# Rounding copies of the spatial weights on ScalarE instead of VectorE, in a fused recurrence and gated-MLP kernel

## The chip, the cores and the metric

The kernel runs on one core of a Trainium2 chip. The metric is the device time of one execution in microseconds (us). The engines of a core have a queue each and work through it in order: TensorE multiplies matrices (in the rows of the profile PE, its weight loads PEld), VectorE is DVE, ScalarE is ACT, GpSimd is POOL, and SyncE (SP) issues the transfers. An instruction that waits holds up everything behind it in the queue of its engine.

## The reference, cut to what matters

A recurrence over 768 tokens for 4 batches and 8 heads, each with a 40 by 40 state, is followed by a gated MLP whose gate mixes tokens with a 768 by 768 matrix, `w_spatial`.

```python
for t in range(S):                                   # S = 768
    y[:, :, t] = np.einsum('bhd,bhde->bhe', rt, state)
    Sa = np.einsum('bhde,bhe->bhd', state, at)
    state = state * wt[:, :, None, :] - np.einsum('bhd,bhe->bhde', Sa, bt) \
            + np.einsum('bhd,bhe->bhde', vt, kt)
x = y.transpose(0, 2, 1, 3).reshape(B, S, H * D)
h = np.maximum(x @ w_in, 0.0)
u, v = h[..., :512], h[..., 512:]
v_n = (v - mu) / np.sqrt(var + 1e-06)
v_s = np.einsum('ts,bsd->btd', w_spatial, v_n) + b_spatial[None, :, None]
return (u * v_s) @ w_out
```

## The kernel before

**First phase.** The recurrence is cut into blocks of 64 tokens. 24 blocks (12 for each of two pairs of batches) go one after the other. Within a block the chain is: product with the state (`c_bp`, matmuls L908) and its copy out of PSUM on ScalarE (`c_bp_out`, L917), a product with the block's triangular matrix (`c_ff`, L925) and its copy (`c_ff_out`, L933), a product with the inverted block matrix (`c_xx`, L946) and its copy (`c_xx_out`, L957), a triangular mask by GpSimd (`strict`, L762), and the new state (`c_mp`, L976, finished on VectorE in L993 and L994) and the output (`c_y`, L1002, L1015). For the block after, ScalarE copies in between what is prepared: `b_lka_out` (`At`, L772), `b_tok_out` (L813), `b_l21_out` (L833), `b_zt_out` (`zt`, L853), `b_xcopy` (L1145). The input layer of the MLP is woven in, 12 units of 128 tokens and two batches: matmuls `m_u` (L1122) and `m_v` (L1076) into the PSUM tiles `pv` and, in the last units, `itmp`; ScalarE's Relu copies `m_u_out` (`ur`, L1128) and `m_v_out` (`vr`, L1082); statistics on VectorE (L1088 to L1106); the normalizing step on ScalarE (`m_n3`, L1111) and the store of `vr` to `vns`. `vr` has two buffers. The order of all of it is written out by hand in a table of numbers, one for each step.

**Second phase.** The spatial product is done with 2 by 2 quadrants in 7 products instead of 8. The weights are needed as 7 quadrants or combinations of quadrants, each split into a rounded part `wsh` and a remainder `wsl`, in fp32r, which TensorE takes. `wprep(i)` makes them for one of three slices of 128 source tokens: a load of `raw` (L311), four differences into `tt` on VectorE (L315), and then four times a rounding copy into `wsh` (L320) and the remainder `wsl` (L321), over 1, 2, 2 and 2 tiles of 384. The three calls are held behind marks in the first phase (places 20.03, 20.51 and 21.68 in units of blocks); from there, and for all that comes after the hand-written part, a scheduler of the framework places each instruction. `raw` has two buffers, which go on to the four chunks of `w_out` (`decode64`, L215 to L255: it makes fp32r pairs `woh` and `wol`) and then to the normalized activations (`vload`, L355, from `vns`). `product` (L402) then does the spatial matmuls, `gate` (L408, L206, L210) the gating and its split, and `proj` (L447, L448) the output layer.

`split_hi` (L206) is the helper that the other splits of the kernel use already; its rows all have line L206.

Of the kernel before, what the change touches and what calls it, by code (L numbers as in the profile page):

```python
# [204 lines left out]
def split_hi(eng, hi, x):  # L205
    eng.activation(hi, x, AF.Copy)  # L206
# [76 lines left out]
def phase2(ctx, tc, vns, uts, wspT, bsp, wout, out, anchors):  # L283
    nc = tc.nc
# [24 lines left out]
    def wprep(i):  # L309
        raw = wstg.tile([P, 2, S], F32, name="raw", bufs=2)  # L310
        nc.sync.dma_start(out=raw, in_=wspT.rearrange("(a k p) t -> k p a t", a=2, p=P)[i])  # L311
        r11, r12, r21, r22 = (raw[:, a, h * TH:(h + 1) * TH] for a in range(2) for h in range(2))
        tt = wstg.tile([P, 4, TH], F32, name="tt")
        for o, x, y in ((0, r12, r11), (1, r22, tt[:, 0]), (2, r22, r12), (3, r21, tt[:, 1])):
            nc.vector.tensor_tensor(out=tt[:, o], in0=x, in1=y, op=ALU.subtract)  # L315
        wh = wsp[2 * i].tile([P, 7, TH], F32R, name=f"wsh{i}")
        wl = wsp[2 * i + 1].tile([P, 7, TH], F32R, name=f"wsl{i}")
        for o, x in ((slice(0, 1), raw[:, 0:1, 0:TH]), (slice(1, 3), raw[:, 1].rearrange("p (h t) -> p h t", h=2)),
                     (slice(3, 5), tt[:, 0:2]), (slice(5, 7), tt[:, 2:4])):
            nc.vector.tensor_copy(out=wh[:, o], in_=x)  # L320
            nc.vector.tensor_tensor(out=wl[:, o], in0=x, in1=wh[:, o].bitcast(F32), op=ALU.subtract)  # L321
        wsh.append(wh)
        wsl.append(wl)

    for i in range(KT):
        sp = mybir.EngineType.SP
        with behind(tc, {**anchors[W_AT[i]], sp: anchors[W_AT[i] - W_LOAD][sp]}):
            wprep(i)
# [1055 lines left out]
```

## Time and profile before

| | us |
|---|---|
| median of 3 runs | 675.8 |
| lowest and highest run | 674.05, 679.77 |
| the profiled execution | 679.68 |
| its span, from the first instruction to the last | 678.0 |
| busy in it: TensorE, VectorE, ScalarE, GpSimd | 581.3, 518.0, 420.3, 208.0 |

How to read it: the profiled execution is one of those that scatter around the median. All times inside it are counted from the start of its span. A row of the timeline gives start, duration (of the whole stretch where several instructions are merged), engine, line, operation, output and input tiles with partitions and elements, the count, and in square brackets the idle time of the engine ahead of it with what ended it. Instructions overlap by their pipelines: the distance between two starts is shorter than the first one's duration. TensorE's granted clock was 1.00 of its full 2.4 GHz in every stretch from 440 us on that is looked at below but the last, with 0.99.

### The profile page before, as it was taken

The page shows a single profiled execution, that of the slowest core. Times are in us where ns is not written, and L with a number is a line of the kernel's source. Part 1 is how long each engine was busy: PE and PEld are TensorE (multiplying, and loading weights), DVE is VectorE, ACT ScalarE, POOL GpSimd, SP SyncE. Part 2 cuts the span into 40 slices and gives each one's busy share as a digit, 9 for nine tenths or more (in the row PEclk, how much of TensorE's full clock was granted, in tenths as well). Part 3 has the DMA queues.
Part 4 walks back from the last instruction along what each step waited for, and adds up shares of the span by engine and source line. Part 5 has one row for each costly group of instructions (what it writes and reads, how often), then busy time and mean ns, then how long its engine had stood idle before and what let it go on. Part 6 is the DMA issues. An engine that isn't in the chain of part 4 may idle for free. (4 is left out here: it accounts for less than half of the span.)

```text
span 678.0 us, 27119 instructions
## 1 busy us (share of the span) xinstructions
PE 581.3 (86%) x11504; PEld 512.6 (76%) x11504; DVE 518.0 (76%) x1110; ACT 420.3 (62%) x934; POOL 208.0 (31%) x286
## 2 busy tenths in 40 slices
PE   1736978878787887997999999989997989999996
PEld 1625866667676676886888888878876989999996
DVE  7871268779988999786899896793498779887842
ACT  3345454538485787786688889888864544443322
POOL 3201030133253445332135342434351113322221
PEclk9976597669796999999899999999999999999999
DMA  8383247276547464474754453655247744544201
GB/s 190 52 155 51 55 95 146 57 125 142 125 92 167 75 147 100 102 160 116 135 132 105 122 145 91 194 143 167 81 123 224 227 160 130 157 133 136 77 30 58
DMA packets 115496, 83.42 MB, mean 123 GB/s; under 512 B 44656, under 2 KB 107376, under 8 KB 113456
## 3 DMA queue, kind: packets, MB, share of 16 engines
q1 hardware_dynamic: 114832, 79.98, 48.4%
q10 hardware_dynamic: 544, 1.72, 1.2%
q8 instruction: 90, 1.47, 1.0%
q14 instruction: 30, 0.25, 0.2%
HBM read 61.16 MB, written 20.50 MB: 120 GB/s over the span
## 5 line engine op out<-in xcount | busy, mean ns | idle before, releaser
L762 POOL TENSOR_SCALAR_AFFINE_SELECT Rt<-Rt 64x256 f32<-64x256 f32 (+1 forms) x144 | 88.4, 615 | 175.9 <-ACT Rt L957 120.7
L762 POOL TENSOR_SCALAR_AFFINE_SELECT At<-At 64x512 f32<-64x512 f32 x48 | 36.1, 752 | 142.8 <-ACT At L772 138.8
L210 POOL TENSOR_TENSOR gl<-g,gh 128x384 fp32r<-128x384 f32 x32 | 34.9, 1091 | 104.2 <-ACT gh L206 104.2
L917 ACT ACTIVATE Rt<-bp 64x416 f32<-64x416 f32 x96 | 49.0, 511 | 23.6 <-PE bp L908 21.6
L957 ACT ACTIVATE Rt<-ch 64x416 f32<-64x416 f32 x96 | 49.1, 511 | 15.0 <-PE ch L946 13.1
L619 DVE TENSOR_TENSOR itmp<-A 128x84 f32<-128x84 f32 (+12 forms) x130 | 53.0, 408 | 2.5
L925 PE MATMUL ch<-Rt,At 128*64 128x104 f32 x768 | 47.3, 264 | 4.1 <-ACT Rt L917 1.8
L623 DVE TENSOR_TENSOR A<-A,itmp 128x84 f32<-128x84 f32 (+12 forms) x130 | 45.0, 346 | 4.5
L925 PEld LDWEIGHTS ch<-Rt,At 128*64 128x64 f32 x768 | 38.3, 141 | 11.1 <-ACT Rt L917 4.5
L946 PE MATMUL ch<-ffs,xf 64*64 64x104 f32 x768 | 39.8, 264 | 5.3 <-ACT ffs L933 4.8
L1015 DVE TENSOR_TENSOR y<-bp,Et 104x256 f32<-104x256 f32 x48 | 19.7, 418 | 32.1 <-ACT zt L853 18.0
L538 DVE TENSOR_TENSOR_SCAN S<-ein,ends 128x528 f32<-128x528 f32 x24 | 30.0, 1250 | 12.9 <-DMA ein<-in_early 9.6
L807 PE MATMUL bk<-ident,sl 128*128 128x128 f32 x192 | 34.6, 311 | 5.9 <-DVE Lc L595 2.4
L946 PEld LDWEIGHTS ch<-ffs,xf 64*64 64x64 f32 x768 | 31.4, 138 | 9.4 <-ACT ffs L933 6.0
L584 PE MATMUL bk<-at,sl 64*32 64x32 f32 x1536 | 21.8, 212 | 17.1 <-DVE sl L571 15.1
L206 ACT ACTIVATE gh<-g 128x384 fp32r<-128x384 f32 x32 | 16.7, 522 | 29.8 <-DVE g L408 29.8
L755 PE MATMUL bk<-at,sl 64*64 64x64 f32 x768 | 33.2, 248 | 1.1 <-issue 1.0
L584 PEld LDWEIGHTS bk<-at,sl 64*32 64x32 f32 x1536 | 18.8, 124 | 20.0 <-DVE sl L571 15.0
L402 PE MATMUL pg<-wsh,hs 128*128 128x384 f32 x96 | 32.3, 337 | 1.3 <-DVE g L408 1.3
L1002 PE MATMUL bp<-Rt,tk 128*40 128x64 f32 x768 | 32.6, 234 | 0.3 <-POOL Rt L762 0.2
L571 DVE TENSOR_TENSOR sl<-ein,S 128x1024 f32<-128x1024 f32 x24 | 30.1, 1255 | 3.6 <-PE bk L807 3.6
L772 ACT ACTIVATE At<-bk 64x512 f32<-64x512 f32 x48 | 28.2, 587 | 6.9 <-PE bk L755 6.2
(186 smaller groups left out, 1743.9 us busy)
## 6 DMA issues: line engine op xcount, KB each, us to landing
ein<-in_early SPq DMA_DIRECT2D x40, 387.0 KB
lin<-in_late SPq DMA_DIRECT2D x48, 160.0 KB
uts<-ur SPq DMA_DIRECT2D x48, 128.0 KB
vns<-vr SPq DMA_DIRECT2D x24, 256.0 KB
ut<-uts SPq DMA_DIRECT2D x48, 128.0 KB
raw<-vns SPq DMA_DIRECT2D x48, 128.0 KB
Rt<-in_vtok SPq DMA_DIRECT2D x48, 80.0 KB
xs<-y SPq DMA_DIRECT2D x48, 80.0 KB
```

Of the source, the lines that this page charges most:

```text
L210: eng.tensor_tensor(out=lo, in0=x, in1=hi.bitcast(F32), op=ALU.subtract)
L584: nc.tensor.matmul(pl[o:o + HB, n, :], lhsT=sl[PR[par], n, par, cs], rhs=at[PR[par], n, cs], start=True, stop=True,)
L619: nc.vector.tensor_tensor(out=tp, in0=A[:, k + 1:, k:k + 1].broadcast_to([P, m, k]), in1=A[:, k:k + 1, 0:k].broadcast_to([P, m, k]), op=AL ...
L623: nc.vector.tensor_tensor(out=A[:, k + 1:, 0:k], in0=A[:, k + 1:, 0:k], in1=tp, op=ALU.add)
L755: nc.tensor.matmul(pk[PR[1 - par], n, :], lhsT=sl[PR[par], n, 1 - par, :], rhs=at[PR[par], n, :], start=True, stop=True,)
L762: nc.gpsimd.affine_select(out=t, in_=t, pattern=[[0, k], [1, C]], base=0, channel_multiplier=-1, compare_op=ALU.is_gt, fill=0.0,)
L807: nc.tensor.transpose(pt[:, n, :], sl[:, h * NP + n].rearrange("p q c -> p (q c)"), ident)
L917: nc.scalar.activation(Rt[par][PR[par], gp, :], st["bp", g][PR[par]], AF.Copy)
L925: nc.tensor.matmul(ff[PR[1 - par], q, :], lhsT=At[par][:, n, :], rhs=Rt[par][:, n, :], start=True, stop=True,)
L946: nc.tensor.matmul(st["xx", g][PR[h ^ flip(s, g)], q, :], lhsT=xf[PR[h], g * NP + q, :], rhs=st["ffs", g][PR[h], q, :], start=True, stop=True,
L957: nc.scalar.activation(Rt[par][PR[par], gp], xx[PR[1 - par ^ flip(s, g)]], AF.Copy, scale=-1.0)
L1002: nc.tensor.matmul(bp[RR[par], q, 0:C], lhsT=tk[:, n, par, :], rhs=Rt[par][:, n, 0:C], start=False, stop=True, skip_group_check=True,)
```

## The change

One call in `wprep` is exchanged. The 12 rounding copies (4 in each of 3 calls) are issued on ScalarE as an activation with the copy function, and the subtraction that gives the remainder stays on VectorE.

```diff
         for o, x in ((slice(0, 1), raw[:, 0:1, 0:TH]), (slice(1, 3), raw[:, 1].rearrange("p (h t) -> p h t", h=2)),
                      (slice(3, 5), tt[:, 0:2]), (slice(5, 7), tt[:, 2:4])):
-            nc.vector.tensor_copy(out=wh[:, o], in_=x)
+            split_hi(nc.scalar, wh[:, o], x)
             nc.vector.tensor_tensor(out=wl[:, o], in0=x, in1=wh[:, o].bitcast(F32), op=ALU.subtract)
```

The scheduler places the new instructions. On GpSimd the order is the same as before. On TensorE and SyncE it is the same up to the last unit of the MLP's input layer, and in the part after it some pieces change places.

ScalarE, at the first call (`wsh_9573` is its output, `bp_7996` and `bp_7997` are the two PSUM tiles of `c_bp`); a piece of the difference:

```order
 L917 ACTIVATE Rt_132<-bp_7996 64x416
 L917 ACTIVATE Rt_133<-bp_7996 64x416
+L206 ACTIVATE wsh_9573<-raw 128x384
+L206 ACTIVATE wsh_9573<-raw 128x768
 L917 ACTIVATE Rt_132<-bp_7997 64x416
 L917 ACTIVATE Rt_133<-bp_7997 64x416
 L1145 ACTIVATE xf_130<-XT_7887 128x8x32
 L1145 ACTIVATE xf_130<-XT_7887 32x8x32 x2
+L206 ACTIVATE wsh_9573<-tt 128x768 x2
 L772 ACTIVATE At_8051<-bk 64x512
 L1097 ACTIVATE q<-q 128x1
```

Two copies now stand between the two pairs of L917, and two more ahead of the copy of `At`. The four copies of the second call stand in the same way between L1111 and L833 a little further on.

ScalarE, at the third call (`wsh_9607`), in the last block of the recurrence; before, and then now:

```order
L933 ACTIVATE ffs<-ch 128x416 x2
L1128 ACTIVATE ur<-pv 128x256
L1111 ACTIVATE vr<-vr,q 128x512
L957 ACTIVATE Rt_134<-ch 64x416
L957 ACTIVATE Rt_135<-ch 64x416
```

```order
L933 ACTIVATE ffs<-ch 128x416 x2
L206 ACTIVATE wsh_9607<-raw 128x384
L206 ACTIVATE wsh_9607<-raw 128x768
L206 ACTIVATE wsh_9607<-tt 128x768 x2
L1128 ACTIVATE ur<-pv 128x256
L1111 ACTIVATE vr<-vr,q 128x512
L957 ACTIVATE Rt_134<-ch 64x416
L957 ACTIVATE Rt_135<-ch 64x416
```

The four copies have moved in ahead of the last block's L957, which was right behind L933, L1128 and L1111.

VectorE, at the third call and the first chunk of `w_out`; before, and then now:

```order
L1106 TENSOR_SCALAR q<-q,mv 128x1
L320 CAST wsh_9607<-raw 128x384
L320 CAST wsh_9607<-raw 128x768
L320 CAST wsh_9607<-tt 128x768 x2
L321 TENSOR_TENSOR wsl_9608<-raw,wsh_9607 128x384
L321 TENSOR_TENSOR wsl_9608<-raw,wsh_9607 128x768
L321 TENSOR_TENSOR wsl_9608<-tt,wsh_9607 128x768 x2
L220 TENSOR_SCALAR tt<-raw 128x320
L225 TENSOR_SCALAR tt<-raw 128x320
L1088 BN_STATS bs<-vr 128x6
```

```order
L1106 TENSOR_SCALAR q<-q,mv 128x1
L321 TENSOR_TENSOR wsl_9608<-raw,wsh_9607 128x384
L321 TENSOR_TENSOR wsl_9608<-raw,wsh_9607 128x768
L321 TENSOR_TENSOR wsl_9608<-tt,wsh_9607 128x768 x2
L220 TENSOR_SCALAR tt<-raw 128x320
L225 TENSOR_SCALAR tt<-raw 128x320
L230 TENSOR_TENSOR tt<-tt 128x320
L232 TENSOR_SCALAR tt<-raw 128x320
L237 SCALAR_TENSOR_TENSOR tt<-tt 128x320
L242 TENSOR_SCALAR tt<-tt 128x320
L247 SCALAR_TENSOR_TENSOR tt<-raw,tt 128x320
L1088 BN_STATS bs<-vr 128x6
```

The four copies are gone, and five more steps of the first chunk's decoding stand ahead of the statistics (L1088), which came after two of them.

## Rows read from the trace of the kernel before

**Rows 1.** The page, its first part: busy time of each engine, share of the span and instructions.

```profile
PE 581.3 (86%) x11504; PEld 512.6 (76%) x11504; DVE 518.0 (76%) x1110; ACT 420.3 (62%) x934; POOL 208.0 (31%) x286
```

**Rows 2.** The table by stretch: length of the stretch, busy time of each engine in it with the count, granted clock, share of the DMA engines, GB/s.

```profile
456.00:500.00 44.00, 42.70 (x924) 36.94 (x921) 23.32 (x66) 36.74 (x84) 19.17 (x25) 1.00 0.43 125
500.00:530.00 30.00, 23.43 (x186) 19.66 (x185) 27.12 (x79) 16.26 (x36) 10.38 (x10) 1.00 0.63 196
550.00:565.00 15.00, 12.92 (x77) 12.22 (x75) 13.39 (x31) 7.10 (x15) 4.49 (x4) 1.00 0.45 143
565.00:678.00 113.00, 107.24 (x650) 105.66 (x648) 78.43 (x133) 41.92 (x89) 29.35 (x27) 0.99 0.32 101
```

**Rows 3.** Groups of instructions by line and shape, VectorE's rounding copies: busy us, mean ns of one, idle time ahead.

```profile
L320 DVE CAST wsh<-tt 128x768 fp32r<-128x768 f32 x6 | 3.6, 620 | 0.0
L320 DVE CAST wsh<-raw 128x768 fp32r<-128x768 f32 x3 | 1.7, 553 | 0.0
L320 DVE CAST wsh<-raw 128x384 fp32r<-128x384 f32 x3 | 1.1, 352 | 0.0
```

**Rows 4.** The timeline of ScalarE: rounding copies of the same shapes that it does already, with the instruction right behind the first.

```profile
506.00 0.83 ACT L206 ACTIVATE xh<-xt 128x768 fp32r<-128x768 f32 x1
506.74 0.37 ACT L1128 ACTIVATE ur<-itmp 128x256 f32<-128x256 f32 x1
...
531.68 0.93 ACT L206 ACTIVATE ha<-raw 128x384 fp32r<-128x384 f32 x2
```

**Rows 5.** The timeline of ScalarE around the first and second call.

```profile
443.13 2.12 ACT L917 ACTIVATE Rt<-bp 64x416 f32<-64x416 f32 x4 [0.37 <-PE bp L908]
445.27 1.15 ACT L1145 ACTIVATE xf<-XT 128x256 f32<-128x256 f32 x3
...
447.43 0.58 ACT L772 ACTIVATE At<-bk 64x512 f32<-64x512 f32 x1
...
448.68 0.93 ACT L933 ACTIVATE ffs<-ch 128x416 f32<-128x416 f32 x2
...
452.95 0.82 ACT L1111 ACTIVATE vr<-vr,q 128x512 f32<-128x512 f32 x1 [1.29 <-DVE q L1106]
453.80 0.78 ACT L833 ACTIVATE l<-bk 32x256 f32<-32x256 f32 x2
454.60 1.58 ACT L957 ACTIVATE Rt<-ch 64x416 f32<-64x416 f32 x3
...
457.23 0.74 ACT L853 ACTIVATE zt<-bk 32x256 f32<-32x256 f32 x2
...
459.95 0.38 ACT L1128 ACTIVATE ur<-pv 128x256 f32<-128x256 f32 x1 [1.49 <-issue]
```

**Rows 6.** The timeline of TensorE: every idle stretch of it (over 0.15 us) from 446 to 500 us, and one `c_y`.

```profile
448.06 1.30 PE L807 MATMUL bk<-ident,sl 128*128 128x128 f32 x8 [0.66 <-ACT At L772]
...
454.23 0.24 PE L844 MATMUL bk<-XT,l 32*32 32x32 f32 x2 [0.37 <-ACT l L833]
454.63 0.69 PE L844 MATMUL bk<-XT,l 32*32 32x32 f32 x30 [0.16 <-ACT l L833]
...
458.03 0.69 PE L872 MATMUL bk<-zt,X 32*32 32x32 f32 x32 [0.76 <-ACT zt L853]
...
459.80 1.09 PE L1002 MATMUL bp<-Rt,tk 128*40 128x64 f32 x32
...
490.56 0.69 PE L872 MATMUL bk<-zt,X 32*32 32x32 f32 x32 [0.28 <-ACT zt L853]
```

**Rows 7.** The timeline of ScalarE at the third call and behind it.

```profile
498.84 1.00 ACT L933 ACTIVATE ffs<-ch 128x416 f32<-128x416 f32 x2
500.53 0.39 ACT L1128 ACTIVATE ur<-pv 128x256 f32<-128x256 f32 x1 [0.68 <-PE pv L1122]
...
512.33 0.82 ACT L1111 ACTIVATE vr<-vr,q 128x512 f32<-128x512 f32 x1 [0.28 <-DVE q L1106]
...
522.36 0.60 ACT L1082 ACTIVATE vr<-pv 128x512 f32<-128x512 f32 x1 [0.23 <-DMA vns<-vr]
```

**Rows 8.** The timeline of TensorE behind the third call.

```profile
504.43 0.61 PE L1122 MATMUL pv<-xh,wh 128*128 128x256 f32 x3 [1.08 <-ACT vr L1082]
...
509.63 0.39 PE L1122 MATMUL itmp<-xh,wh 128*128 128x256 f32 x1 [0.53 <-POOL xh L210]
...
523.01 0.62 PE L1122 MATMUL pv<-xh,wh 128*128 128x256 f32 x3 [2.29 <-ACT vr L1082]
```

**Rows 9.** The timeline of VectorE at the third call and the first step of the decoding.

```profile
499.59 0.82 DVE L320 CAST wsh<-raw 128x384 fp32r<-128x384 f32 x2
500.33 1.02 DVE L320 CAST wsh<-tt 128x768 fp32r<-128x768 f32 x2
501.26 1.42 DVE L321 TENSOR_TENSOR wsl<-raw,wsh 128x384 fp32r<-128x384 f32 x2
...
504.46 0.42 DVE L220 TENSOR_SCALAR tt<-raw 128x320 int32<-128x320 int32 x1
```

**Rows 10.** The timeline of GpSimd: four masks while VectorE does copies of the second call, and four in the next but one block.

```profile
455.18 2.85 POOL L762 TENSOR_SCALAR_AFFINE_SELECT Rt<-Rt 64x256 f32<-64x256 f32 x4 [6.09 <-ACT Rt L957]
...
488.45 1.84 POOL L762 TENSOR_SCALAR_AFFINE_SELECT Rt<-Rt 64x256 f32<-64x256 f32 x4
```

**Rows 11.** The timeline of SyncE's queue: the first loads of the normalized activations.

```profile
525.14 3.12 SPq L355 DMA_DIRECT2D raw<-vns  x5
```

## The prediction

> **What bounds the kernel now.** I read the page first: TensorE is busy for 581.3 us of the span, ahead of VectorE's 518.0 and ScalarE's 420.3 [rows 1]. That is a mean; the edit touches only the stretch from about 444 to 504 us, where the three calls stand. So the table by stretch came next [rows 2]. From 456 to 500 us TensorE is busy for 42.70 of 44.00 us and ScalarE for 36.74, VectorE for only 23.32. From 500 to 530 us it is VectorE, with 27.12 of 30.00, while TensorE has 30.00 - 23.43 = 6.57 us idle. From 565 us to the end TensorE works through without long gaps (107.24 of 113.00). So the end comes when TensorE's queue is through: idle time that is added to TensorE ahead of 565 us is added to the end, unless idle time further on shrinks for it. Last I read the timelines of ScalarE, TensorE and VectorE around the calls [rows 5 to 9], because a mean doesn't say who waits. What the reader is to see in rows 6: every wait of TensorE from 446 to 500 us (they sum to 2.2 us) was ended by ScalarE, none by VectorE.
>
> **What the change removes.** Twelve copies leave VectorE, 3.6 + 1.7 + 1.1 = 6.4 us of busy time [rows 3]. By starts it is less: the four of the third call occupy VectorE from 499.59 to 501.26, so 1.67 us [rows 9], and three calls free 5.0 us.
>
> **What it adds.** ScalarE's copy of 128x768 takes 0.83 us, and the next instruction starts 0.74 us after it; two of 128x384 take 0.93 us, the last one's duration being 0.53, so the first occupies 0.40 [rows 4]. A call has one of 384 and three of 768: 0.40 + 3 x 0.74 = 2.62 us, and three calls 7.9 us. No transfer is added, and the load of `raw` is the same.
>
> A rule of the Trainium skill speaks against the change: the page Perfetto Trace Analysis, section Optimizing Scalar/DVE Operations, says that where VectorE has a faster mode for an operation it beats ScalarE, and that handing work to ScalarE may pay if VectorE is saturated. The trace agrees with the first half, with 0.55 us against 0.83 for 128x768 [rows 3, 4].
>
> **First and second call: +3.9 us.** The first call's copies stand two ahead of the second pair of L917 and two ahead of the copies of `At`. ScalarE has no idle time from 443.13 to beyond 448.68 that could hide them [rows 5], so the second copy of `At` moves from 447.43 to 450.05. TensorE's L807 waited for just this one, at 448.06 [rows 6]; behind it the whole queue stands, the recurrence included, and it starts 2.6 us later. ScalarE's next idle time is the 1.29 us ahead of L1111, which waits for VectorE's `q` [rows 5]. `q` stands behind the remainders of the first call; VectorE has 1.67 us less to do there, so this wait goes and takes up 1.3 us. Then the second call adds 2.62 us. Together 2 x 2.62 - 1.3 = 3.9 us for what follows on ScalarE: L833 (453.80), L957 (454.60) and `zt` (457.23) [rows 5]. TensorE waited for L833 at 454.23 and 454.63, and for `zt` at 458.03 [rows 6]; these starts move by 3.9 us too. ScalarE's 1.49 us idle ahead of L1128 at 459.95 takes nothing back: it stands behind a matmul that is late by as much. From 458 to 500 us TensorE has one wait left, of 0.28 us [rows 6]; the delay stays. Bounds: 2.6 us if the second call were hidden, 5.2 us if nothing is.
>
> VectorE's 3.3 us less in these two calls bring nothing else that I find: TensorE waited for VectorE nowhere here [rows 6], and VectorE has room [rows 2].
>
> A second rule bears on GpSimd. First the rows: four masks took 2.85 us beside the second call's copies, and 1.84 us at 488.45 [rows 10], so 1.0 us more. Their outputs are wanted by L1002, which started at 459.80 [rows 6], 1.8 us after the last mask's end at 458.03: shorter masks move nothing. The Trainium skill, page SBUF — State Buffer, section on the two separate sides, says that VectorE's two-port copies lock GpSimd out of their shared port for a whole instruction. By that rule GpSimd gains the 1.0 us with this change, and the sum would be 1.0 us lower if it were on the path; by the rows it isn't.
>
> **Third call: +1.2 us.** Its copies stand behind L933 at 498.84, whose second one ends at 499.84, and ahead of L1128 at 500.53, which had 0.68 us idle time before it [rows 7]: 2.62 - 0.68 = 1.94 us later are L1128, the last block's L957, and `vr` (L1082), for which TensorE waited at 504.43 [rows 8]. VectorE gains little: its remainders must now wait for ScalarE's copies. Those would end at about 500.4, 501.1, 501.8 and 502.5. The four remainders took 504.46 - 501.26 = 3.20 us [rows 9]; begun at 500.4, with a short wait for the second copy, they end at 503.8. The decoding of `w_out` starts then, against 504.46 [rows 9]: 0.65 us earlier, not 1.67. (These times leave out the 3.9 us.) Behind that the pace is set by the loop of the two `vr` buffers: copy, statistics, normalizing (L1111, which waited for VectorE at 512.33), store, next copy (L1082, which waited for the store at 522.36) [rows 7]. I let the 0.53 us for which TensorE waited for GpSimd at 509.63 [rows 8] and a little of VectorE's lead take back 0.7 of the 1.94 us: +1.2. Bounds: nothing, if the 6.57 us of idle time swallow it; 1.94 + 2.29 = 4.2 us if the new order of the tail adds one more wait as long as the longest there [rows 8].
>
> **Sum.** 3.9 + 1.2 = 5.1 us: the profiled span of 678.0 becomes 683.1. That execution took 679.68 us, above the median of 675.8; the difference carried to the median gives 675.8 + 5.1 = 680.9 us, 0.8% slower.
>
> **Rivals.**
> 1. *The tail swallows it.* TensorE's 6.57 us of idle time from 500 to 530 us [rows 2] take the place of the delay. For it: this idle time is partly waits for transfers, which need not move. Against it: the units that wait there are fed by the recurrence's end and by ScalarE, both late. With 1 us left over it gives 676.8.
> 2. *VectorE was the bound of the tail, and the kernel gets faster.* The place is 500 to 530 us: the four chunks of `w_out` hold the `raw` buffers that the first L355 at 525.14 needs [rows 11], VectorE is 90% busy [rows 2], the decoding's first chunk stands ahead of the statistics now, and the third chunk's load stands earlier on SyncE. If the products start so early that all 6.57 us are filled: 675.8 + 3.9 - 6.6 = 673.1. It decides from 3.9 us taken back on. Against it: L355 follows stores of the `vr` loop on SyncE, and the loop's copy at 522.36 waited for a store, not for VectorE. The half-sentence on a saturated VectorE in the page Perfetto Trace Analysis of the Trainium skill points to this rival.
> 3. *The new order of the tail stalls.* A piece of the last unit's matmuls stands earlier among the products, and TensorE waits in order. One more wait of 2.29 us, with the 1.94 us unabsorbed: 675.8 + 3.9 + 4.2 = 683.9.
> 4. *GpSimd was on the path*: 680.9 - 1.0 = 679.9. The rule of the page SBUF — State Buffer is behind this one; the rows speak against the path, not against the shorter masks.
>
> **Chances.** Forecast 0.45, rival 1 0.2, rival 2 0.1, rival 3 0.2, rival 4 0.05. The likeliest is 680.9 us, and its own range 678.4 (lower bound of the two calls, nothing in the tail) to 683.0 (5.2 + 2). With the rivals 673 to 686: the low end is rival 2, the high end rival 3 with the 5.2 us. The runs shown spread over 5.7 us, so about 1% (6.8 us) is what a measurement can tell from no change. Slower by more than that, above 682.6, is rival 3 and the upper end of the forecast, 0.27; faster by more, below 669.0, would take more than rival 2, 0.04; 0.69 remain within 1%.
>
> **What would show it.** No L320 rows; L206 writing `wsh` on ScalarE, 12 times, about 0.83 us for 768. TensorE's wait ahead of L807 at 448 grows from 0.66 to about 3 us, and the waits ahead of L844 and L872 sum to about 1.3 us more. The L933 of the last block, at 498.84 before, is about 3.9 us later. TensorE's L1122 at 504.43 starts near 510.3, the first L355 (525.14) near 530.2. VectorE's remainders show waits for ScalarE in the third call. If that L933 isn't late, the step on the first two calls is wrong; if it is and the end isn't, rival 1 or 2 holds; if the idle time from 500 to 530 us grows by over 2 us, rival 3.

## The result, and the profile after

With the change the kernel took 684.86 us, the median of 12 runs, beside 679.66 us for 12 runs of the kernel before on the same chip: ratio 1.0089, 95% interval 1.0063 to 1.0114. On the 675.8 us of the forecast that is 6.0 us slower (4.3 to 7.7); 5.1 us were forecast. The forecast started from 675.8 us, the median of three of these twelve runs of the kernel before. Carried to that start the measured 6.0 us give 681.8, inside the forecast's own range of 678.4 to 683.0; the 684.86 as measured lie above that range, and inside the one with the rivals, 673 to 686. The ratios here and below leave out runs in a slower state (over 1.5% above the fastest of their kernel), the medians keep them, and this can shift a ratio by 0.8% (e9 below: 1.0163, from its medians of 684.36 and 678.87 us 1.0081).

The profiled execution took 682.63 us, its span is 680.9, against 678.0 before. This difference of 2.9 us must not be read as the price: the start of the first L917 behind the first call's place is at 441.15 us here and at 443.13 before, and nothing is changed ahead of it. So the traces are compared from there on, in stretches that end with an L917: the next block's, the last block's, the first L355 (the second phase's first load), and the end. The table by stretch, of the kernel before (length, busy time of TensorE, its weight loads, VectorE, ScalarE and GpSimd with counts, granted clock, DMA share, GB/s):

```profile
443.13:462.33 19.20, 17.13 (x400) 14.53 (x396) 17.76 (x41) 15.96 (x37) 5.78 (x8) 1.00 0.60 175
462.33:496.19 33.86, 33.45 (x731) 28.93 (x725) 15.15 (x42) 28.46 (x66) 15.96 (x20) 1.00 0.36 100
496.19:525.14 28.95, 22.97 (x205) 19.32 (x206) 26.17 (x81) 17.38 (x38) 8.24 (x8) 1.00 0.62 192
525.14:678.00 152.86, 144.43 (x869) 140.70 (x867) 111.20 (x218) 61.97 (x133) 36.99 (x34) 0.99 0.39 123
```

and of the changed one:

```profile
441.15:465.21 24.06, 19.45 (x400) 16.99 (x396) 13.68 (x33) 21.66 (x46) 4.57 (x8) 0.86 0.49 141
465.21:499.08 33.87, 33.46 (x731) 28.94 (x725) 15.14 (x42) 28.46 (x66) 15.98 (x20) 1.00 0.36 99
499.08:529.54 30.46, 24.28 (x214) 20.39 (x214) 28.19 (x82) 19.99 (x43) 6.38 (x8) 1.00 0.56 178
529.54:680.90 151.36, 144.15 (x861) 141.18 (x860) 108.17 (x211) 61.29 (x132) 38.26 (x34) 0.99 0.40 125
```

The first stretch, with the first two calls, is 4.86 us longer; the second is the same; the third, with the third call, is 1.51 longer; and the rest is 1.50 shorter: 4.88 us in all. So in these two traces the first two calls make all of it, and the third call's delay is given back behind the first L355. In the first stretch TensorE does the same 400 matmuls but is busy for 19.45 us instead of 17.13, at a mean clock of 0.86: something besides waiting was lost.

ScalarE's timeline in the first stretch, after (answers to [rows 5]):

```profile
441.15 1.05 ACT L917 ACTIVATE Rt<-bp 64x416 f32<-64x416 f32 x2 [0.38 <-PE bp L908]
442.22 1.26 ACT L206 ACTIVATE wsh<-raw 128x384 fp32r<-128x384 f32 x2
443.50 1.05 ACT L917 ACTIVATE Rt<-bp 64x416 f32<-64x416 f32 x2
...
445.74 1.58 ACT L206 ACTIVATE wsh<-tt 128x768 fp32r<-128x768 f32 x2
...
448.46 0.58 ACT L772 ACTIVATE At<-bk 64x512 f32<-64x512 f32 x1
...
452.81 0.38 ACT L1128 ACTIVATE ur<-pv 128x256 f32<-128x256 f32 x1 [0.24 <-PE pv L1122]
453.22 0.81 ACT L1111 ACTIVATE vr<-vr,q 128x512 f32<-128x512 f32 x1
453.94 1.24 ACT L206 ACTIVATE wsh<-raw 128x384 fp32r<-128x384 f32 x2
455.08 1.57 ACT L206 ACTIVATE wsh<-tt 128x768 fp32r<-128x768 f32 x2
456.67 0.78 ACT L833 ACTIVATE l<-bk 32x256 f32<-32x256 f32 x2
```

Counted from the first L917, the second copy of `At` starts at 448.46 - 441.15 = 7.31 us; before it was 447.43 - 443.13 = 4.30 [rows 5]: 3.01 later. L1128 is then 3.51 later (11.66 against 451.28 - 443.13 = 8.15), L1111 2.25 (12.07 against 9.82; its wait of 1.29 us for `q` is gone), L833 4.85 (15.52 against 10.67). TensorE's timeline beside it (answers to [rows 6]):

```profile
449.10 1.97 PE L807 MATMUL bk<-ident,sl 128*128 128x128 f32 x8 [3.57 <-ACT At L772]
450.72 0.99 PE L1122 MATMUL pv<-xh,wh 128*128 128x256 f32 x3
...
457.50 0.69 PE L844 MATMUL bk<-XT,l 32*32 32x32 f32 x30 [0.16 <-ACT l L833]
...
460.90 0.69 PE L872 MATMUL bk<-zt,X 32*32 32x32 f32 x32 [0.76 <-ACT zt L853]
```

The wait ahead of L807 is 3.57 us. Behind it the same eight matmuls took 1.97 us, against 1.30 [rows 6], and at 449 us the granted clock is on the lower of its two levels, 1.2 instead of 2.4 GHz. The table by stretch shows for how long (clock in the third column from the right):

```profile
446.00:449.00 3.00, 0.00 (x0) 0.00 (x0) 2.31 (x5) 2.93 (x7) 0.96 (x1) 0.80 0.62 170
449.00:454.00 5.00, 4.91 (x56) 4.62 (x60) 2.59 (x7) 4.55 (x13) 0.65 (x1) 0.50 0.50 119
454.00:455.00 1.00, 1.00 (x32) 0.88 (x24) 0.00 (x0) 1.00 (x3) 0.00 (x0) 0.67 0.58 186
455.00:458.00 3.00, 2.84 (x44) 2.06 (x40) 0.00 (x0) 2.91 (x6) 0.00 (x0) 1.00 0.93 279
```

VectorE's remainders wait for ScalarE's copies now, and the decoding starts behind them (its timeline; answers to [rows 9]):

```profile
446.62 1.83 DVE L321 TENSOR_TENSOR wsl<-tt,wsh 128x768 fp32r<-128x768 f32 x2 [0.74 <-ACT wsh L206]
...
503.17 0.56 DVE L321 TENSOR_TENSOR wsl<-raw,wsh 128x384 fp32r<-128x384 f32 x1 [0.61 <-ACT wsh L206]
...
506.64 0.33 DVE L220 TENSOR_SCALAR tt<-raw 128x320 int32<-128x320 int32 x1
```

### The profile page after: what moved, and what is told of

Read it like the earlier page. It is cut to its first block, busy times and chain, and to the rows that moved or that the text cites. A ratio compares the mean times of both kernels' runs of the same rounds, so it can differ in the third digit from the quotient of the medians.

```text
span 680.9 us, 27127 instructions
## 1 busy us (share of the span) xinstructions
PE 580.7 (85%) x11504; PEld 514.2 (76%) x11504; DVE 515.1 (76%) x1098; ACT 427.7 (63%) x946; POOL 204.4 (30%) x286
## 3 DMA queue, kind: packets, MB, share of 16 engines
q10 hardware_dynamic: 544, 1.72, 1.2%
## 5 line engine op out<-in xcount | busy, mean ns | idle before, releaser
L762 POOL TENSOR_SCALAR_AFFINE_SELECT Rt<-Rt 64x256 f32<-64x256 f32 (+1 forms) x144 | 85.5, 594 | 177.1 <-ACT Rt L957 113.7
L917 ACT ACTIVATE Rt<-bp 64x416 f32<-64x416 f32 x96 | 49.0, 511 | 27.9 <-PE bp L908 26.0
L957 ACT ACTIVATE Rt<-ch 64x416 f32<-64x416 f32 x96 | 49.0, 511 | 12.1 <-PE ch L946 10.1
L925 PE MATMUL ch<-Rt,At 128*64 128x104 f32 x768 | 48.7, 269 | 4.2 <-ACT Rt L917 2.0
L807 PE MATMUL bk<-ident,sl 128*128 128x128 f32 x192 | 32.7, 300 | 9.0 <-ACT At L772 4.9
L206 ACT ACTIVATE hs<-tt 128x384 fp32r<-128x384 f32 x32 | 16.7, 524 | 27.6 <-PE pg L402 16.3
L807 PEld LDWEIGHTS bk<-ident,sl 128*128 128x128 f32 x192 | 22.3, 150 | 13.9 <-ACT At L772 5.5
```

Source lines behind the costliest of these rows:

```text
L762: nc.gpsimd.affine_select(out=t, in_=t, pattern=[[0, k], [1, C]], base=0, channel_multiplier=-1, compare_op=ALU.is_gt, fill=0.0,)
L807: nc.tensor.transpose(pt[:, n, :], sl[:, h * NP + n].rearrange("p q c -> p (q c)"), ident)
L917: nc.scalar.activation(Rt[par][PR[par], gp, :], st["bp", g][PR[par]], AF.Copy)
L925: nc.tensor.matmul(ff[PR[1 - par], q, :], lhsT=At[par][:, n, :], rhs=Rt[par][:, n, :], start=True, stop=True,)
L957: nc.scalar.activation(Rt[par][PR[par], gp], xx[PR[1 - par ^ flip(s, g)]], AF.Copy, scale=-1.0)
```

## The experiments

Each kernel was profiled once. This table gives for each profile the start of the first L917 behind the first call's place, of the next block's and of the last block's, and the span; then A, from the first L917 to the next block's, and C, from the last block's to the end (span less its start); and the ratio to the kernel before with its interval, where it was timed. In some kernels L917 is a few lines further down.

| kernel | first | next | last | span | A | C | ratio |
|---|---|---|---|---|---|---|---|
| before | 443.13 | 462.33 | 496.19 | 678.0 | 19.20 | 181.81 | |
| the change | 441.15 | 465.21 | 499.08 | 680.9 | 24.06 | 181.82 | 1.0089 (1.0063 to 1.0114) |
| e1, calls 1 and 2 | 441.56 | 465.30 | 499.20 | 680.3 | 23.74 | 181.10 | 1.0130 (1.0085 to 1.0174) |
| e2, call 3 | 445.51 | 464.73 | 498.60 | 679.4 | 19.22 | 180.80 | 1.0016 (0.9978 to 1.0053) |
| e6, call 1 | 441.50 | 463.45 | 497.33 | 679.1 | 21.95 | 181.77 | |
| e7, call 2 | 438.13 | 461.87 | 495.75 | 678.6 | 23.74 | 182.85 | |
| e3, both engines copy | 439.52 | 461.30 | 495.95 | 679.2 | 21.78 | 183.25 | 1.0109 (1.0068 to 1.0149) |
| e4, filled wait | 443.22 | 468.89 | 502.78 | 683.4 | 25.67 | 180.62 | 1.0111 (1.0057 to 1.0164) |
| e5, the change at other marks | 445.30 | 466.24 | 501.54 | 681.3 | 20.94 | 179.76 | 1.0061 (1.0025 to 1.0097) |
| e8, xf on VectorE | 444.51 | 466.60 | 502.19 | 685.3 | 22.09 | 183.11 | 1.0056 (1.0020 to 1.0092) |
| e9, call 3 twice on ScalarE | 438.63 | 462.22 | 496.11 | 679.8 | 23.59 | 183.69 | 1.0163 (1.0074 to 1.0252) |
| e10, remainders 3 twice | 440.49 | 464.13 | 498.01 | 681.5 | 23.64 | 183.49 | 1.0140 (1.0067 to 1.0213) |
| e11, three vr buffers | 442.73 | 461.95 | 495.82 | 676.8 | 19.22 | 180.98 | 1.0004 (0.9964 to 1.0044) |
| e12, before at the marks of e5 | 444.67 | 462.63 | 497.19 | 678.4 | 17.96 | 181.21 | 0.9913 (0.9869 to 0.9957) |

The first column spreads over 7.4 us, from 438.13 (e7) to 445.51 (e2), though only e5, e11 and e12 have anything changed ahead of it; this alone is 1.1% of the time. A scatters by 0.5 us over four profiles with the same edit there (the change, e1, e9, e10), C by 1.75 us over the four kernels with nothing changed behind the last L917 (before, e1, e6, e7: 181.10 to 182.85). In nine of the eleven timed kernels the ratio asks for more than the trace shows from the first L917 to the end (e1: 1.0130 is 8.8 us, its trace is 3.87 longer). So the argument rests on A and C, and the ratios give the direction.

**e1 and e2: which calls cost.** e1 puts ScalarE's copies into the first two calls only, e2 into the third only:

```diff
-            split_hi(nc.scalar, wh[:, o], x)
+            if i < 2:      # e2: if i == 2
+                split_hi(nc.scalar, wh[:, o], x)
+            else:
+                nc.vector.tensor_copy(out=wh[:, o], in_=x)
```

> Only the first two calls' copies go to ScalarE; the third call's stay on VectorE. Theory A (the copies hold up ScalarE's queue ahead of At and L833, TensorE waits for them and then runs at a lower clock for a while): the stretch from the first row of L917 behind the first call's mark to the L917 of the next block is 24 us as in the changed kernel, against 19.2 before; the run is 4 to 6 us slower than before, ratio 1.006 to 1.009. Theory B (the third call and the new order of the tail carry the loss): ratio 0.998 to 1.002, and the stretch still may be longer, but is given back by 530 us.

> Only the third call's copies go to ScalarE. Theory A: the stretch between the two rows of L917 is 19.2 us as before, the last block's L957 is about 1.9 us later against its L933, and of this 0 to 1.5 us reach the end: ratio 0.999 to 1.003. Theory B: ratio 1.006 to 1.010, all of the loss.

A is 23.74 us in e1 and 19.22 in e2, as in the change and as before: the first two calls make the delay of that stretch, 4.4 to 4.9 us over the four profiles with it. By the runs, e2 can't be told from no change, and the intervals of e1 and of the change overlap. e1's ratio is above the 1.006 to 1.009 that were expected, and its trace doesn't say why.

**e6 and e7: one call each.** As e1, with `if i == 0` and `if i == 1`.

> Only the first call's copies are on ScalarE. The stretch from the first L917 behind the call's mark to the first L917 of the next block was 19.20 us before and 24.06 with the whole change. Theory (ScalarE's queue, a lower clock of TensorE behind the long wait, and the wait for q that takes some of it up): the wait ahead of L807 is the long one again, about 3.6 us, the clock falls behind it, and what ScalarE is late by is partly taken up ahead of L1111; 19.20 + 2.6 + 1.0 - 1.3 = 21.5 us, 21.0 to 22.3. Rival (each copy simply costs its time, nothing is taken up, and the clock costs nothing): 19.20 + 2.4 = 21.6, the same sum, but with L807's wait at 3.3 us and a clock of 1.00. Rival (the second call alone makes the delay, since the first one is hidden by VectorE's earlier q): under 20.2.

> Only the second call's copies are on ScalarE. Theory: L807's wait stays at about 0.7 us and the clock at 1.00, L1111 waits for q about 1.3 us as before, and the copies delay L833 by their 2.6 to 2.8 us: 19.20 + 2.7 = 21.9 us for the stretch, 21.4 to 22.4. Rival (the whole of the extra 1 us over the forecast came in the second call, by VectorE's remainders or longer copies, and not from the clock behind the first): 22.6 or more. Rival (TensorE's other work ahead of L833 hides half of it): under 21.0.

The first call alone costs 21.95 - 19.20 = 2.75 us, inside what the theory gave, and the wait and the lower clock came with it, which speaks against the rival of the same sum (the granted clock is 0.52 from 449.50 to 451.50 us). TensorE's row, where L810 is L807 elsewhere, then ScalarE's, where L836 is L833:

```profile
449.46 1.92 PE L810 MATMUL bk<-ident,sl 128*128 128x128 f32 x8 [3.58 <-ACT At L775]
```

```profile
454.38 0.78 ACT L836 ACTIVATE l<-bk 32x256 f32<-32x256 f32 x2
```

L836 starts 12.88 us behind the first L917, 2.21 later than before; the other 0.54 us is TensorE, which from L810 to L1005 has no wait over 0.15 us any more and is itself the chain.

The second call alone was expected to cost 2.7 and cost 4.54. That is the number of its first rival, but not by the rival's cause. ScalarE's part came as expected: the copies stand between L1111 and L833 (here L836), which starts 451.41 - 438.13 = 13.28 us behind the first L917, 2.61 later than before. What was missed lies behind it, on TensorE (its timeline, then the table by stretch):

```profile
451.84 0.24 PE L847 MATMUL bk<-XT,l 32*32 32x32 f32 x2 [2.98 <-ACT l L836]
...
458.71 1.71 PE L1005 MATMUL bp<-Rt,tk 128*40 128x64 f32 x32
```

```profile
452.00:453.00 1.00, 0.84 (x36) 0.72 (x36) 0.00 (x0) 0.95 (x3) 0.21 (x1) 1.00 1.07 321
453.00:459.00 6.00, 6.00 (x110) 5.51 (x110) 2.60 (x7) 3.13 (x8) 2.10 (x5) 0.52 0.40 130
```

A wait of 2.98 us, and from 453 us on the lower clock: L1005 (L1002 elsewhere) took 1.71 us, against 1.09 at 459.80 before [rows 6]. 4.54 - 2.61 = 1.93 us were lost at the lower clock. Both calls alone sum to 2.75 + 4.54 = 7.29 us, together they cost 4.86: with the first call delayed too, TensorE comes to L844 late itself and waits there 0.16 us, so the second wait and its lower clock don't come.

**e4: the wait filled.** The change, with twelve matmuls of 128x512 whose result nobody reads, ahead of the L807 that waits:

```diff
-        sl = st["pre", s][2]
+        sl = st["pre", s][2]; fill(ps_i.tile([P, DH], F32, name="itmp")) if (s, h) == (21, 0) else None
...
+    def fill(z): [nc.tensor.matmul(z, lhsT=wh[:, 0, 0:P], rhs=wh[:, 0, DH:], start=True, stop=True) for _ in range(12)]
```

> The changed kernel with 12 more matmuls of 128x512 into an unused PSUM tile on TensorE, right ahead of the L807 that waits for ScalarE; about 3.2 us of work in the 3.6 us of the wait. Nothing reads them. If the lower clock behind the wait is due to the wait and costs time: the clock stays at 1.00 from 449 to 455 us, L807 takes 1.3 us and not 2.0, and the stretch between the two L917 rows falls from 24.1 to 22.7 to 23.3 us, so the run is about 1 us faster than the changed kernel. If the clock has nothing to do with the loss: the stretch stays at 24.1 us or gets longer. The tail's order differs a little, so only the stretch decides, not the total.

At the filled place the theory held: the clock stayed up (1.00 from 449 to 455 us) and L807 took its 1.30 us again. But the stretch is 25.67 us, longer than with the change, where 22.7 to 23.3 were expected. TensorE's timeline:

```profile
451.19 1.30 PE L807 MATMUL bk<-ident,sl 128*128 128x128 f32 x8 [0.62 <-ACT At L772]
...
458.71 0.24 PE L844 MATMUL bk<-XT,l 32*32 32x32 f32 x2 [1.72 <-ACT l L833]
...
465.51 1.94 PE L1002 MATMUL bp<-Rt,tk 128*40 128x64 f32 x32
```

TensorE was faster through its next matmuls, came to L844 early and waited 1.72 us for ScalarE; behind that wait the clock fell (mean 0.69 from 458 to 468.89 us), now ahead of L1002, on which the next block hangs. L833 started 458.28 - 443.22 = 15.06 us behind the first L917, 0.46 earlier than with the change; so the lower clock behind L807 costs the change only this half microsecond, and ScalarE's queue the rest.

**e3: no relief for VectorE.** ScalarE makes the copies in addition, into the place that the remainder then overwrites, and VectorE still makes its own:

```diff
-            split_hi(nc.scalar, wh[:, o], x)
+            split_hi(nc.scalar, wl[:, o], x)
+            nc.vector.tensor_copy(out=wh[:, o], in_=x)
```

> ScalarE makes the twelve copies in addition, into the place that the remainder overwrites, and VectorE still makes its own, so VectorE is not relieved and its remainders still stand behind ScalarE. Theory (VectorE's relief takes up some of the delay, at L1111 in the first two calls and in the decoding in the third): the stretch is 0.5 to 1.5 us longer than with the change, 24.6 to 25.6, and the kernel 0.2 to 0.4% slower than the change: ratio to before 1.011 to 1.013. Rival (VectorE's 5.0 us bring nothing at all): stretch 24.1, ratio 1.009. Rival (VectorE's relief is worth its full 5 us): ratio 1.016 or more.

The scheduler put ScalarE's copies of the second call two blocks further down, to 490.35 us, so the expected stretch doesn't apply, and the ratio says nothing on VectorE's relief. The first call can be compared with e6, and there the relief is worth nothing that the scatter of 0.5 us would show: A is 21.78 us with VectorE's own copies and 21.95 without them. ScalarE's row shows why; L1111 (here L1112) doesn't wait for `q` either:

```profile
451.39 0.82 ACT L1112 ACTIVATE vr<-vr,q 128x512 f32<-128x512 f32 x1
```

**e5 and e12: the place of the calls.** e5 is the change with later marks, e12 the kernel before with the same marks:

```diff
-W_AT = (20.03, 20.51, 21.68)
+W_AT = (20.76, 21.76, 22.76)
```

> The changed kernel with the marks of the three calls moved from 20.03, 20.51 and 21.68 to 20.76, 21.76 and 22.76: the first two calls' copies now stand on ScalarE ahead of the L1128 for which it has 1.5 us idle time; the third call's stand where they stood. Theory A (the price is that of the place): each of the first two calls costs 2.62 - 1.5 = 1.1 us in place of 4.9 together, TensorE has no wait over 1 us there and its clock stays; the kernel is 0 to 3 us slower than before, ratio 1.000 to 1.005. If ScalarE's time itself is the price wherever it stands: 1.006 to 1.010 as now.

> The kernel before (VectorE makes the copies) with the three marks at 20.76, 21.76 and 22.76, the places that the change was also run with. There, with ScalarE's copies, the three blocks' stretches were longer by 1.74, 1.70 and -0.26 us, TensorE's L908 waited 2.78 us for VectorE's y (L1015) behind the first call, and the time from the last block's first L917 to the end was 179.8 us against 181.8. Theory (y was late because VectorE's remainders, which stand ahead of it in order, waited for ScalarE's copies): with VectorE's own copies y is late by less than 1 us, the stretches are longer by 0 to 1 us in sum, and the ratio to before is 0.996 to 1.001. Rival (the place itself is bad: 6 to 8 us of VectorE's work of any kind ahead of y): L908 waits 2 us or more again, the sum of the stretches is 2 to 4 us longer, ratio 1.002 to 1.006.

In e5 the last L917 comes 501.54 - 445.30 = 56.24 us behind the first, 3.18 more than before (53.06) and 1.69 less than with the change (57.93); C is 2.05 us shorter, little more than its scatter. That the calls cost less between other blocks holds, but the expectation of no wait over 1 us and a full clock doesn't: a new wait came, for VectorE's `y`, which stands behind remainders that wait for ScalarE, and behind it the clock fell (mean 0.72 from 464 to 470 us). With VectorE's own copies, in e12, TensorE has no wait over 0.15 us at that place, behind the first call, and its longest wait for `y` comes one block further on, behind the second. TensorE's rows for the longest wait for `y`, of e5 and then of e12:

```profile
464.57 0.40 PE L908 MATMUL bp<-lin,Mc 40*64 40x104 f32 x4 [2.78 <-DVE y L1015]
```

```profile
477.93 0.40 PE L908 MATMUL bp<-lin,Mc 40*64 40x104 f32 x4 [0.89 <-DVE y L1015]
```

From the first to the last L917, e12 takes 52.52 us, 0.54 less than before, so the theory on `y` holds. Its runs gave 674.41 us against 678.97 for before, ratio 0.9913: of all kernels tried the only one whose interval lies below 1, and by more than was expected. From the first L917 to the end its trace shows only 234.87 - 233.73 = 1.1 us; its 7 runs lie between 670.19 and 681.84 us. That it is faster is what the interval says; how much of the 0.9% is more than scatter ahead of the first L917 stays open.

**e8: the opposite direction.** The kernel before, with the copies to `xf` (L1145) of the last four blocks moved from ScalarE to VectorE:

```diff
-N16, JB, JX, CPV, XCV, LKV, HV = 1, 16, 16, 14, 99, 99, 99
+N16, JB, JX, CPV, XCV, LKV, HV = 1, 16, 16, 14, 20, 99, 99
```

> The opposite direction: in the kernel before, the copies XT to xf (L1145) of the blocks from 20 on go from ScalarE to VectorE, some 1.0 us of ScalarE's queue per block in four blocks; the twelve rounding copies stay on VectorE. Theory (ScalarE is what TensorE waits for from 446 to 500 us and VectorE has room): TensorE's 2.2 us of waits for ScalarE there shrink, the kernel is up to 2.2 us faster: ratio 0.997 to 1.000, stretch of 19.20 at 18.2 to 19.2. Rival (VectorE does things in order, so the copies wait there behind casts and remainders, and TensorE waits for xf): 1 to 3 us slower, ratio 1.001 to 1.005. Rival (ScalarE was no bound at all): no difference, and the copies of the change cost by something else than ScalarE's queue.

The ratio is that of the first rival, and the cause is VectorE's order as it said, but TensorE doesn't wait for `xf`. VectorE has room on the average; the copies stand in its queue between the first calls' work, and `q` comes later. ScalarE's row, then TensorE's, and the table by stretch behind it:

```profile
455.24 0.81 ACT L1111 ACTIVATE vr<-vr,q 128x512 f32<-128x512 f32 x1 [3.99 <-DVE q L1106]
```

```profile
456.50 0.24 PE L844 MATMUL bk<-XT,l 32*32 32x32 f32 x2 [2.18 <-ACT l L833]
```

```profile
456.50:460.00 3.50, 3.34 (x94) 3.07 (x96) 3.47 (x7) 3.37 (x8) 2.27 (x4) 0.73 0.81 192
460.00:465.00 5.00, 4.97 (x82) 4.52 (x76) 3.18 (x9) 2.24 (x6) 0.79 (x1) 0.51 0.42 158
```

ScalarE, relieved, waits 3.99 us for VectorE instead of 1.29; TensorE then waits 2.18 us for ScalarE and falls to the lower clock. L833 starts 456.08 - 444.51 = 11.57 us behind the first L917, only 0.90 later than before; the other 1.99 of the 2.89 us by which A grew are lost behind that wait, at the lower clock. Ahead of the last L917 TensorE waits once more for VectorE, 2.05 us for `y`.

**e9 to e11: what the tail hides.** e9 makes the third call's copies twice on ScalarE, e10 its remainders twice on VectorE, both on top of the change; e11 is the kernel before with three buffers for `vr`:

```diff
+            if i == 2:                       # e9, ahead of the copy
+                split_hi(nc.scalar, wl[:, o], x)
...
+            if i == 2:                       # e10, behind the remainder
+                nc.vector.tensor_tensor(out=wl[:, o], in0=x, in1=wh[:, o].bitcast(F32), op=ALU.subtract)
...
-        vr = st["act"].tile([P, DH], F32, name="vr", bufs=2)
+        vr = st["act"].tile([P, DH], F32, name="vr", bufs=3)
```

> The change, with the third call's four copies made twice by ScalarE (first into the place that the remainder overwrites): 2.62 us more on ScalarE, and VectorE's remainders 2.6 us later. From the last block's first L917 to the end it was 181.81 us before and 181.82 with the change. Theory (the tail behind it has so much idle time that ScalarE's third call costs nothing at the end): 180.5 to 182.8 again, the kernel at the change's ratio of about 1.009. Rival (the third call costs what the prediction gave, 1.2 us, and only the scatter of that one run hid it): with twice the copies 1.9 + 2.6 less 0.7, so 185 to 186, ratio 1.013 or more.

> The change, with the third call's four remainders computed twice: about 3.2 us more on VectorE from 503 us on, which was busy for 27.12 of the 30 us from 500 to 530. Theory (the tail is paced by the loop of the two vr buffers and their stores, not by VectorE): at most 1 us of it shows, 181 to 183 us from the last block's first L917 to the end. Rival (VectorE is the bound of the tail): all of it shows, 184.5 to 185.5, ratio 1.013.

> The kernel before with three buffers for vr instead of two; VectorE makes the copies as before. TensorE waited for ScalarE's vr (L1082) four times from 500 to 530 us, 1.08 + 1.59 + 2.29 + 0.59 = 5.55 us, and L1082 itself waited for the store of vr at 515.30 and 522.36. Theory (the loop of the two vr buffers paces the tail): these waits shrink by 2 to 5 us, the time from the last block's first L917 to the end falls from 181.8 to 177 to 180, ratio 0.993 to 0.997. Rival (the tail's idle time is taken by transfers and by what hangs on the last recurrence, not by these buffers): 181 to 183, ratio 1.000. Rival (the new order that three buffers bring stalls elsewhere): ratio 1.002 or more.

C is 183.69 us in e9 and 183.49 in e10, each between what its theory and its rival gave. Beside the change's 181.82 that is 1.87 us more for the 2.62 added on ScalarE, and 1.67 more for the 3.2 added on VectorE. But the three kernels with the third call once on ScalarE (the change, e2, e4) lie between 180.62 and 181.82, so up to 3.07 and 2.87 us may show; and in both traces TensorE's clock fell in the tail (mean 0.72 from 504 to 510 us in e9, behind a wait of 4.07 us, and 0.72 from 526 to 532 in e10, behind 2.18), which it didn't with the change. What the added work costs by itself is therefore not separated. The tail hid the third call once and seems to let much of a second one through; which engine bounds it isn't shown. In e11 TensorE's waits for `vr` fall from 5.55 us to 1.35 (1.09 and 0.26), and others take their place (TensorE's timeline):

```profile
516.66 0.96 PE L1076 MATMUL pv<-wh,xh 128*128 128x512 f32 x3 [1.19 <-ACT ur L1128]
...
552.21 0.54 PE L402 MATMUL pg<-wsh,hs 128*128 128x384 f32 x1 [2.10 <-DVE g L408]
```

C is 180.98 us, within its scatter, and the ratio is 1.0004: the theory that the loop of the two `vr` buffers paces the tail falls.

## Why the prediction was right, point by point

**The bound was named rightly.** TensorE's queue, fed by ScalarE from 446 to 500 us, turned the copies into delay; e1 and e2 put it where the prediction did. The total of 5.1 us lies in the measured 4.3 to 7.7. But two terms were off in opposite directions, 1 us too low and 1.2 too high, and their errors cancel: that the sum came out so close is luck. The end of the range with the rivals was added up wrongly, since rival 3 with the 5.2 us makes 685.2 and not 686; nothing hangs on it.

**First and second call: 3.9 us forecast, 4.86 in the trace of the change** (4.4 to 4.9 over four profiles), below the upper bound of 5.2. From ScalarE's starts: 3.01 us at the second copy of `At` against 2.62 (the copies take 1.28 + 1.60 us from start to start, 0.26 more than worked out from [rows 4], and 0.13 is elsewhere); then 0.50 that the prediction didn't have, since TensorE works at the lower clock behind the wait of 3.57 us and ScalarE waits for it; then -1.26 at L1111 against -1.3; then 2.60 for the second call against 2.62. These sum to 4.85. e4 sizes the clock's part by itself at 0.46 us. The sign that was named came: the last block's L933 starts 501.73 - 441.15 = 60.58 us behind the first L917, against 498.84 - 443.13 = 55.71 [rows 7], 4.87 later.

**The wait for `q` goes, but not for the reason given.** The prediction let it go because VectorE has less to do. In e3 VectorE has no less to do, and L1111 doesn't wait either: ScalarE simply comes later than `q`. That "VectorE's 3.3 us less in these two calls bring nothing else" was right, and could have been said of all of it.

**The waits ahead of L844 and L872 didn't grow.** Forecast were 1.3 us more; they fell, from 0.37 + 0.16 + 0.76 us [rows 6] to 0.16 + 0.76, because TensorE was late itself. Where the second call stands alone (e7), the wait is there, 2.98 us, and costs more than its length.

**Third call: 1.2 us forecast, nothing left at the end.** Up to the first L355 the working held. ScalarE's rows for L933 and L1128, then SyncE's for the first L355:

```profile
501.73 1.00 ACT L933 ACTIVATE ffs<-ch 128x416 f32<-128x416 f32 x2
...
505.24 0.37 ACT L1128 ACTIVATE ur<-pv 128x256 f32<-128x256 f32 x1
```

```profile
529.54 1.85 SPq L355 DMA_DIRECT2D raw<-vns  x4
```

L1128 starts 505.24 - 499.08 = 6.16 us behind the last L917, against 500.53 - 496.19 = 4.34 [rows 7]: 1.82 later, 1.94 forecast. The decoding starts 7.56 us behind it, against 504.46 - 496.19 = 8.27 [rows 9]: 0.71 earlier, 0.65 forecast. The first L355 is 1.51 later, counted from the last L917. Then 1.50 us come back, of which 1.22 are idle time of TensorE behind that L355: 152.86 - 144.43 = 8.43 us before, 151.36 - 144.15 = 7.21 after. The failed step is "a little of VectorE's lead take back 0.7 of the 1.94": it looked for the cover only ahead of 530 us. With C scattering by 1.75 us, nothing means here -1 to +1 us, and e9 suggests that little cover is left.

**The rivals.** Rival 1, the tail swallows the delay, came true for the third call alone; it didn't for the first two, since with e1, where only these are changed, C is 181.10 us against 181.81 before and A is 4.54 us longer. Rival 2, VectorE as the bound of the tail, stays open by e10 (1.67 us or more of 3.2 show), but its condition, that the change takes 3.9 us back, isn't met. Rival 3 didn't come: the idle time of TensorE from the last L917 to the first L355 is 30.46 - 24.28 = 6.18 us, against 28.95 - 22.97 = 5.98. Rival 4: GpSimd's four masks are shorter without VectorE's copies beside them, 2.02 us against 2.85 [rows 10]:

```profile
458.05 2.02 POOL L762 TENSOR_SCALAR_AFFINE_SELECT Rt<-Rt 64x256 f32<-64x256 f32 x4 [8.29 <-ACT Rt L957]
```

L1002, which needs them, starts at 462.67, 2.6 us behind their end at 460.07; they are still not on the path. The Trainium skill, page SBUF — State Buffer, section on the two separate sides, says that a two-port operation of VectorE locks GpSimd out of the port that they share; the shorter masks agree with it.

## What to carry to other kernels

Ask not which engine has the lower busy share, but what stands behind the new instruction in its queue and who waits for that: in the first stretch VectorE was busy for 17.76 of 19.20 us and ScalarE for 15.96, and moving work from the busier to the less busy one still made the stretch 4.86 us longer, as moving other work the opposite way (e8) made it 2.89 longer, most of that by the clock. A wait on the engine that bounds the kernel can cost more than its length when its clock falls behind it, and the same wait filled or removed may only move the loss to a worse place (e4, e7). Delays on one chain don't add up, and small edits are best read in a trace from the first instruction that they can touch, since here the part ahead of it scattered by more than the whole effect.

## What the runs showed of the hardware

The price of the lower clock depends on what stands behind it. It fell behind waits of TensorE of 1.72 us (e4), 2.18 (e8), 2.78 (e5), 2.98 (e7) and 3.57 (the change), and not behind the 0.66 and 0.76 us of the kernel before. The length of the wait alone doesn't decide it: in the tail the granted clock stayed at 1.00 behind 2.29 us in the kernel before [rows 8], 2.62 in e1 and 2.69 in e12, and fell to 0.50 behind 2.07 in e7 and 2.35 in e2. What decides isn't shown here. Behind the 3.57 us it cost the chain 0.5 us, since ScalarE set the pace of the next matmuls (e6, where TensorE was the chain up to the next block, lost 0.54 behind the like wait); behind the 2.98 us it cost 1.93, since the matmuls up to the next block's start (L1002: 1.71 us instead of 1.09) were themselves the chain. The Trainium skill, page TensorE: Matmul & The Clock Gate, Part 1, describes a clock of two rates that falls to the half one when the engine idles; the clock of 0.50 in these rows agrees.
